# Attention and two MLPs on one core: a third exponentials buffer, selects for first tiles, one bias product a bank

## The chip, the core and the metric

One core of a Trainium2 chip runs the whole program. The metric is device time in microseconds; lower is better. Engines are named as in the profile: PE (TensorE), DVE (VectorE), ACT (ScalarE), POOL (GpSimd) and SP (SyncE, which issues every load and store here).

## What is computed

Four batches, eight heads, 576 positions, head size 64. The attention is banded (128 positions back) with a linear bias; its output, 2304 tokens by 512, goes through two MLPs with 2048 hidden units, the first with a rational activation, the second with SiLU.

```python
scores = scale * np.matmul(q, k.transpose(0, 1, 3, 2))      # scale = 1/8
bias = slopes[:, None, None] * (-np.abs(rel))[None]         # slopes 2**-(h+1)
mask = (rel >= 0) & (rel < 128)
attn = softmax(where(mask, scores + bias, -1e9))
x = (attn @ v) as 2304 x 512
h = x @ w_in;  g = P(h) / (Q(h) + 1e-6);  x = g @ w_out      # P cubic, Q quadratic in |h|
h = x @ w2_in; g = h / (1 + exp(-h));     out = g @ w2_out
```

## The kernel before, in words

The 2304 tokens are 18 tiles of 128. The first MLP works on five blocks of 4, 4, 3, 4 and 3 tiles (`BLK1`). For each block the attention runs as four groups, one for each pair of heads; group `gi` is pair `gi % 4` of block `gi // 4`, so groups 0 to 3 are all that block 0 needs, and groups 4 to 7 belong to block 1.

A group goes through these steps (`group`, below). A tile of 128 queries is cut into halves of a group (two tiles each). S: PE multiplies q and k into two PSUM banks, one for each head of the pair (line 727); a band of 128 behind a tile reaches into the tile before, so the scores lie in two 128-column parts, and DVE folds them into one by a masked copy (`copy_predicated`, line 741). In block 0, apart from the first half of group 0, PE has laid the bias and the band's mask into the bank beforehand, as a product of a scaled identity and a table (`bias_mm`, line 712); there DVE takes the row maximum (line 757) and ACT the exponential (line 762). Everywhere else DVE adds a scaled table `tabs` and takes the maximum in one custom instruction (line 750), which writes the tile `e`, and ACT takes the exponential in place (line 774). A sequence's first tile (tiles 0 and 9 lie at such a start) has no tile before it and uses a variant of the table. Then come the sums' reciprocals (lines 785, 786), the normalising product on POOL or DVE (line 793), transposes by PE (line 813), masks that split the transposed weights into the own and the previous tile (lines 844 to 862, into the tile `ph`), AV by PE (line 890), and the splitting of the result into a high and a low part, `xh` and `xl`, which the MLP reads (lines 905 to 914).

`e` has `OPT['eb']` = 2 buffers and `ph` has `OPT['ptb']` = 1; the q and k tiles have 3 each. A buffer comes free when the last reader of the group that holds it is done: for `e` its transposes, for `ph` its AV.

In `step`, one of the 16 hidden slices of a block goes through `h` (lines 948 to 950), an elementwise chain on ACT and DVE, a split into `gh` and `gl`, and the second product (lines 1017 to 1019). The weights arrive as 64-bit floats and are rebuilt by ACT and DVE (lines 573 to 580), then split into a high part (`whi`, line 470 or 478) and a low part (`wlo`, line 489 on POOL). The second MLP (`phase_a`, `phase_b`) uses a scheme with seven products in place of eight on combined quarters.

The order of the instructions on every engine is made ahead of time. Each operation is given to a planner, `Plan`, with a priority, an engine or several to choose from (`'act|pool'`), a cost and what it reads and writes. `Plan.schedule` walks through planned time and picks for each engine the ready operation with the lowest priority value; buffers and PSUM banks count as resources. `SHIFTS` then moves the priorities of runs of operations, by their index in the list. The numbers in `OPT` set the priorities of whole kinds of work (`dS`, `dT`, `dA` of S, transposes and AV; `qlead` and `vlead` of loads). The engines run the resulting order and wait for each other by semaphores. Where the plan has PE idle near the start, filler matmuls of the identity are put in (`spin`, line 517; `warm`, `fill`).

## Time and profile before

| | us |
|---|---|
| median of 3 runs (lowest to highest) | 870.12 (869.34 to 870.36) |
| profiled execution, its own time | 869.87 |
| its span, first to last instruction | 868.1 |
| PE busy | 855.8 (99%) |
| DVE busy | 674.0 (78%) |
| POOL busy | 638.1 (74%) |
| ACT busy | 579.5 (67%) |

The span is the time between the first and the last instruction of the profiled execution; the execution's own time has a little around it. Busy shares of engines overlap, and they are means over stages that differ: the first 56 us (loads, the attention of block 0, no MLP yet), the first MLP with the attention of later blocks beside it up to about 500 us, and the second MLP. The granted clock of PE is 1.00 over the span. In a timeline, consecutive instructions of the same kind are merged into one row with a count, and the brackets show how long the engine had been idle and what the profile takes for the releaser.

### The profile page before, as it was taken

The page shows a single profiled execution, that of the slowest core. Times are in us where ns is not written, and L with a number is a line of the kernel's source. Part 1 is how long each engine was busy: PE and PEld are TensorE (multiplying, and loading weights), DVE is VectorE, ACT ScalarE, POOL GpSimd, SP SyncE. Part 2 cuts the span into 40 slices and gives each one's busy share as a digit, 9 for nine tenths or more (in the row PEclk, how much of TensorE's full clock was granted, in tenths as well). Part 3 has the DMA queues.
Part 4 walks back from the last instruction along what each step waited for, and adds up shares of the span by engine and source line. Part 5 has one row for each costly group of instructions (what it writes and reads, how often), then busy time and mean ns, then how long its engine had stood idle before and what let it go on. Part 6 is the DMA issues. An engine that isn't in the chain of part 4 may idle for free.

```text
span 868.1 us, 15306 instructions
## 1 busy us (share of the span) xinstructions
PE 855.8 (99%) x5082; PEld 766.2 (88%) x5082; DVE 674.0 (78%) x1336; ACT 579.5 (67%) x1235; POOL 638.1 (74%) x615
## 2 busy tenths in 40 slices
PE   8899999999999999999999999999999999999998
PEld 6677787877788998777899999999999999999998
DVE  7899988799999898998889985567855577655662
ACT  5799997799888998988889884235422355222451
POOL 5778844676889898779899666479954599744894
PEclk9999999999999999999999999999999999999999
DMA  7566674587789877976797989898888888978884
GB/s 252 170 226 202 202 274 132 169 285 253 274 322 313 304 272 262 309 275 231 267 346 237 291 285 333 302 320 281 278 278 252 289 295 282 292 246 263 249 270 164
DMA packets 80462, 228.94 MB, mean 264 GB/s; under 512 B 8192, under 2 KB 17152, under 8 KB 80384
## 3 DMA queue, kind: packets, MB, share of 16 engines
q1 hardware_dynamic: 80384, 227.98, 78.8%
q8 instruction: 40, 0.66, 0.3%
q14 instruction: 38, 0.31, 0.1%
HBM read 178.66 MB, written 49.28 MB: 263 GB/s over the span
## 4 chain that ended last, share of the span: by engine, by line
PE 79%; DVE 9%; ACT 5%; POOL 3%; issue 2%; DMA 1%; SPq 0%; POOLq 0%; DVEq 0%; ACTq 0%
PE acc L1017 6%; PE h L948 6%; PE acc L1019 5%; PE acc L1018 5%; PE h L950 5%; PE h L949 5%; PE z_b L1360 4%; PE z_b L1358 4%; PE z_b L1359 4%; PE z_a L1294 4%; PE z_a L1292 4%; PE z_a L1293 4%; PE bank_atA L890 2%; PE bank_atA L727 2%; PE bank_atB L1358 1%
## 5 line engine op out<-in xcount | busy, mean ns | idle before, releaser
L489 POOL TENSOR_TENSOR xl_b<-g,xh_b 128x384 fp32r<-128x384 f32 x87 | 97.3, 1121 | 70.9 <-DVE xh_b L474 61.2
L1017 PE MATMUL acc<-gh,wo 128*128 128x512 f32 (+1 forms) x320 | 121.5, 380 | 0.0
L1019 PE MATMUL acc<-gl,wo 128*128 128x512 f32 (+1 forms) x320 | 118.5, 370 | 0.1
L1018 PE MATMUL acc<-gh,wo 128*128 128x512 f32 (+1 forms) x320 | 117.9, 368 | 0.0
L470 ACT CAST xh_b<-g 128x384 fp32r<-128x384 f32 x137 | 70.3, 515 | 67.9 <-PE z_b L1360 41.7
L485 DVE TENSOR_TENSOR xl_b<-g,xh_b 128x384 fp32r<-128x384 f32 x81 | 86.2, 1070 | 24.2 <-ACT xh_b L470 23.3
L389 ACT ACTIVATE g<-t_a 128x384 f32<-128x384 f32 x72 | 37.9, 527 | 93.3 <-DVE t_a L382 93.3
L489 POOL TENSOR_TENSOR gl<-t,gh 128x512 fp32r<-128x512 f32 (+1 forms) x73 | 89.8, 1230 | 13.0 <-ACT gh L470 8.7
L489 POOL TENSOR_TENSOR g<-g,g 128x384 f32<-128x384 f32 x72 | 84.5, 1183 | 2.1
L948 PE MATMUL h<-xh,ws 128*128 128x512 f32 (+1 forms) x224 | 83.9, 374 | 0.1
L950 PE MATMUL h<-xh,ws 128*128 128x512 f32 (+1 forms) x224 | 82.2, 367 | 0.0
L949 PE MATMUL h<-xl,ws 128*128 128x512 f32 (+1 forms) x224 | 82.0, 366 | 0.0
L1017 PEld LDWEIGHTS acc<-gh,wo 128*128 128x128 f32 x320 | 60.0, 188 | 13.8 <-issue 5.7
L1019 PEld LDWEIGHTS acc<-gl,wo 128*128 128x128 f32 x320 | 60.0, 188 | 9.4 <-DVE gl L485 0.7
L1018 PEld LDWEIGHTS acc<-gh,wo 128*128 128x128 f32 x320 | 60.2, 188 | 6.6
L1294 PE MATMUL z_a<-xf,w2s 128*128 128x384 f32 x192 | 64.2, 334 | 0.0
L1292 PE MATMUL z_a<-xf,w2s 128*128 128x384 f32 x192 | 64.1, 334 | 0.0
L1293 PE MATMUL z_a<-xf,w2s 128*128 128x384 f32 x192 | 64.1, 334 | 0.0
L1358 PE MATMUL z_b<-xh_b,wo2s 128*128 128x384 f32 x192 | 64.1, 334 | 0.0
L1359 PE MATMUL z_b<-xl_b,wo2s 128*128 128x384 f32 x192 | 64.1, 334 | 0.0
L1360 PE MATMUL z_b<-xh_b,wo2s 128*128 128x384 f32 x192 | 64.1, 334 | 0.0
L964 ACT ACTIVATE t<-h,ab 128x512 f32<-128x512 f32 (+1 forms) x72 | 46.7, 649 | 20.4 <-PE h L950 19.9
(227 smaller groups left out, 2732.4 us busy)
## 6 DMA issues: line engine op xcount, KB each, us to landing
w2s<-forms_w SPq DMA_DIRECT2D x84, 512.0 KB, 4.6
wo2s<-forms_wo SPq DMA_DIRECT2D x84, 512.0 KB, 4.6
ws<-sc SPq DMA_DIRECT2D x64, 512.0 KB, 4.5
raw_w<-in_w SPq DMA_DIRECT2D x32, 512.0 KB, 4.9
raw_wo<-in_wo SPq DMA_DIRECT2D x32, 512.0 KB, 5.4
forms_w<-st_w SPq DMA_DIRECT2D x24, 512.0 KB, 5.5
forms_wo<-st_wo SPq DMA_DIRECT2D x24, 512.0 KB, 4.7
sc<-w SPq DMA_DIRECT2D x16, 512.0 KB, 5.6
```

The source lines that it names most:

```text
L489: nc.gpsimd.tensor_tensor(out=o, in0=a, in1=b, op=op)
L948: nc.tensor.matmul(o, lhsT=T[W][:, 0, c], rhs=xh, start=kt == 0, stop=False)
L949: nc.tensor.matmul(o, lhsT=T[W][:, 0, c], rhs=xl, start=False, stop=False)
L950: nc.tensor.matmul(o, lhsT=T[W][:, 1, c], rhs=xh, start=False, stop=kt == KD - 1)
L1017: nc.tensor.matmul(a, lhsT=T[WO][:, 0, c], rhs=T[G1][:, :n], start=first_f, stop=False)
L1018: nc.tensor.matmul(a, lhsT=T[WO][:, 1, c], rhs=T[G1][:, :n], start=False, stop=False)
L1019: nc.tensor.matmul(a, lhsT=T[WO][:, 0, c], rhs=T[G2][:, :n], start=False, stop=last_f)
L1292: nc.tensor.matmul(o, lhsT=w(0, kt * P), rhs=x[:, 0, kt], start=st and kt == 0, stop=False, skip_group_check=True)
L1293: nc.tensor.matmul(o, lhsT=w(0, kt * P), rhs=x[:, 1, kt], start=False, stop=False, skip_group_check=True)
L1294: nc.tensor.matmul(o, lhsT=w(1, kt * P), rhs=x[:, 0, kt], start=False, stop=kt == 1, skip_group_check=True)
L1358: nc.tensor.matmul(o, lhsT=w(0, m * P), rhs=h, start=st and q == 0, stop=False, skip_group_check=True)
L1359: nc.tensor.matmul(o, lhsT=w(0, m * P), rhs=l, start=False, stop=False, skip_group_check=True)
```

## The change

`e` gets a third buffer. Its 4 KB a partition are taken from `tabs`, which held four tables a head and now holds three: the variant for first tiles goes. Where the fused add read that variant, a first tile's scores are now set to -1e30 outside the own triangle by one more masked copy (a constant column added to `lnb`), and the ordinary table is added. The order of the tables in the input changes with it, so that the product that lays bias and mask into a bank can be one matmul of 512 columns for each head instead of one of 256 for each tile. The first loads of q and k become separate operations. The choices of engines, the numbers in `OPT` and the whole list `SHIFTS` are set anew.

```diff
-    'wlo': 'pool',
+    'wlo': 'dve|pool',
...
-    'eb': 2,
+    'eb': 3,
...
-    'tabs': 'pool',
+    'tabs': 'act|pool',
...
-    'dS': -1.447,
-    'dT': 0.007,
-    'dA': 0.316,
+    'dS': -1.436,
+    'dT': 0.056,
+    'dA': 0.277,
...
-    'look': 1.601,
+    'look': 0.404,
...
-    'dg': -0.473,
+    'dg': -2.41,
...
-    'warm': 3,
+    'warm': 4,
...
-    'vlead': -0.148,
-    'qlead': 0.132,
+    'vlead': 6.85,
+    'qlead': 39.155,
...
-    'alt': 2,
+    'alt': 0,
...
-    's1': 'act|dve',
+    's1': 'act',
...
-    'th': 'act|dve',
+    'th': 'act|dve|pool',
...
-    'idn': 'dve',
+    'idn': 'pool',
...
 SHIFTS = [
-    (4, 3, -0.36), (50, 1, -0.49), (163, 60, 0.42), (297, 3, 0.9),
...
+    (31, 6, 0.69), (73, 20, -0.43), (172, 55, 0.56), (250, 20, 0.18),
...
@@ -499,8 +500,8 @@
         ident = const.tile([P, P], F32, name="ident")
         na = const.tile([P, 4], F32, name="na")
         ab = const.tile([P, 2], F32, name="ab")
-        lnb = const.tile([P, 2], F32, name="lnb")
-        tabs = tab_p.tile([P, H, 4, P], F32, name="tabs")
+        lnb = const.tile([P, 3], F32, name="lnb")
+        tabs = tab_p.tile([P, H, 3, P], F32, name="tabs")
         tabr = tab_p.tile([P, 2, 2, P], F32R, name="tabr")
         slope = tab_p.tile([P, HP, P], F32R, name="slope")
 
@@ -508,6 +509,7 @@
         make_identity(nc, ident)
         nc.vector.memset(lnb[:, 0:1], C * 2.0 ** -63)
         nc.vector.memset(lnb[:, 1:2], -LN2_63)
+        nc.vector.memset(lnb[:, 2:3], -1e30)
 
     pl.op(-99, "pool", 600, k_ident, writes=[("ident", 0), ("lnb", 0)])
 
@@ -530,8 +532,8 @@
             pl.op(-91.0 + 0.5 * part, "sp", 1150, lambda cols=cols: nc.sync.dma_start(tab_all[:, cols], table[:, cols]), writes=[("tab", part)])
         for part in range(2):
             for h in range(H):
-                pl.op(-70 + 0.1 * h + 10 * (h // 2) + 25 * part, do_copy("act" if h + part == 0 else OPT["tabs"], 2 * P,
-                      lambda h=h, part=part: (tabs[:, h, 2 * part:2 * part + 2], tab[:, 4 * part:4 * part + 2]), scale=-8.0 * 2.0 ** -(h + 1)), 0, None,
+                pl.op(-70 + 0.1 * h + 10 * (h // 2) + 25 * part, do_copy("act" if h + part == 0 else OPT["tabs"], (1 + part) * P,
+                      lambda h=h, part=part: (tabs[:, h, part:1 + 2 * part], tab[:, (1, 4)[part]:(2, 6)[part]]), scale=-8.0 * 2.0 ** -(h + 1)), 0, None,
                       reads=[("tab", part)], writes=[("tabs", h, part)])
         for hh in range(2):
             pl.op(-80.5 + 0.1 * hh, do_copy(("dve", "act")[hh], 2 * P, lambda hh=hh: (tabr[:, hh], tab[:, 0:2]), scale=0.5 ** hh), 0, None, reads=[("tab", 0)], writes=[("tabr", hh)])
@@ -623,7 +625,7 @@
 
 
     FIRST = (0, 9)
-    TABLE = {0: 1, 9: 1, 4: 2, 13: 2, 5: 3, 14: 3}
+    TABLE = {0: 0, 9: 0, 4: 2, 13: 2, 5: 3, 14: 3}
     blk_start = [sum(BLK1[:i]) for i in range(len(BLK1))]
     groups = [(bi, hp) for bi in range(len(BLK1)) for hp in range(HP)]
     xkey = {}
@@ -642,15 +644,16 @@
 
         if gi == 0:
 
-            def first(lo, hi):
+            def first(tag, d, src, lo, hi):
+                if not lo:
+                    T[(tag, gi)] = qk_p.tile([P, NB1MAX + d, P], F32, tag=tag, name=f"{tag}{gi}")
+                nc.sync.dma_start(T[(tag, gi)][:, lo + d:hi + d], src[hp, :, lo * P:hi * P].rearrange("p (t c) -> p t c", c=P))
+
+            for a, (lo, hi) in enumerate(((0, 2), (2, n))):
                 for tag, d, src in (("kd", 1, kn), ("qd", 0, qn)):
-                    if not lo:
-                        T[(tag, gi)] = qk_p.tile([P, NB1MAX + d, P], F32, tag=tag, name=f"{tag}{gi}")
-                    nc.sync.dma_start(T[(tag, gi)][:, lo + d:hi + d], src[hp, :, lo * P:hi * P].rearrange("p (t c) -> p t c", c=P))
-
-            pl.op(p, "sp", 2 * DMA_TILE * 2, lambda: first(0, 2), writes=[("kd", gi, 0), ("qd", gi, 0)])
-            pl.op(p + 1.5, "sp", 2 * DMA_TILE * (n - 2), lambda: first(2, n), writes=[("kd", gi, 1), ("qd", gi, 1)])
-            pl.ops[-1].deps -= set(pl.tile_ops[("kd", gi)])
+                    pl.op(p + 1.5 * a + 0.01 * (1 - d), "sp", DMA_TILE * (hi - lo), lambda tag=tag, d=d, src=src, lo=lo, hi=hi: first(tag, d, src, lo, hi), writes=[(tag, gi, a)])
+                    if a:
+                        pl.ops[-1].deps -= set(pl.tile_ops[("kd", gi)]) | set(pl.tile_ops[("qd", gi)])
         else:
             pl.op(p, "sp", DMA_TILE * (n + pv), load("kd", qk_p, NB1MAX + 1, ks, kn), writes=[("kd", gi)])
             pl.op(p, "sp", DMA_TILE * n, load("qd", qk_p, NB1MAX, slice(0, n), qn), writes=[("qd", gi)])
@@ -708,10 +711,9 @@
             def bias_mm(S_=S_, half=half, open_s=open_s):
                 open_s()
                 for hh in range(2):
-                    for i in half:
-                        nc.tensor.matmul(T[S_[hh]][:, i % 2], lhsT=slope[:, hp],
-                                         rhs=tabr[:, hh, TABLE.get(tiles[i], 0):TABLE.get(tiles[i], 0) + 1].broadcast_to([P, 2, P]),
-                                         start=i % 2 == 0, stop=False)
+                    t_ = tabr[:, hh] if half[0] == 0 else tabr[:, hh, 1:2].broadcast_to([P, 2, P])
+                    nc.tensor.matmul(T[S_[hh]].rearrange("p t (k c) -> p t k c", c=P), lhsT=slope[:, hp],
+                                     rhs=t_.unsqueeze(2).broadcast_to([P, 2, 2, P]), start=True, stop=False)
 
             def s_mm(S_=S_, half=half, by_pe=by_pe, open_s=open_s):
                 if not by_pe:
@@ -734,7 +736,7 @@
 
                 pl.op(pH - 0.4 * w, do_copy(OPT["qs"], len(half) * P, q_scaled, scale=0.125), 0, None, reads=[("qd", gi, a)] if gi == 0 else [("qd", gi)],
                       writes=[("qd", gi, a)])
-                pl.op(pH - 0.01 * w, "pe", 60 + 2 * len(half) * c_pe(2 * P), bias_mm, reads=[("tabr", 0), ("tabr", 1), ("slope", hp)], writes=list(S_))
+                pl.op(pH - 0.01 * w, "pe", 30 + 2 * c_pe(4 * P), bias_mm, reads=[("tabr", 0), ("tabr", 1), ("slope", hp)], writes=list(S_))
             pl.op(pH, "pe", 210 + sum(c_pe4(P if k0[i] else 192) for i in half), s_mm, reads=[("kd", gi, a), ("qd", gi, a)] if gi == 0 else [("kd", gi), ("qd", gi, a) if by_pe else ("qd", gi)], writes=list(S_))
             if two:
                 for hh in range(2):
@@ -742,12 +744,19 @@
                         T[S_[hh]][:, two, c1], tab[:, 2:3].bitcast(U32).broadcast_to([P, nt_, P]), T[S_[hh]][:, two, 0:P]),
                         reads=[("tab", 0)], writes=[S_[hh]])
 
+            for i in half:
+                if k0[i] and not by_pe:
+                    for hh in range(2):
+                        pl.op(pH + (0.021 + 0.005 * hh) * w, "dve", c_dve(P), lambda hh=hh, S_=S_, i=i: nc.vector.copy_predicated(
+                            T[S_[hh]][:, i % 2:i % 2 + 1, c1], tab[:, 2:3].bitcast(U32), lnb[:, 2:3].unsqueeze(2).broadcast_to([P, 1, P])),
+                            reads=[("tab", 0), ("lnb", 0)], writes=[S_[hh]])
+
             def mx(i, hh, S_):
                 if M_ not in T:
                     new_ml()
                 if E_ not in T:
                     new_et()
-                nc.vector.tensor_tensor_reduce(out=T[E_][:, i, hh], in0=T[S_[hh]][:, i % 2, c1], in1=tabs[:, 2 * hp + hh, TABLE.get(tiles[i], 0)],
+                nc.vector.tensor_tensor_reduce(out=T[E_][:, i, hh], in0=T[S_[hh]][:, i % 2, c1], in1=tabs[:, 2 * hp + hh, max(TABLE.get(tiles[i], 1) - 1, 0)],
                                                scale=-0.125, scalar=3.0e38, op0=ALU.add, op1=ALU.min, accum_out=T[M_][:, i, hh:hh + 1])
 
             if by_pe:
@@ -776,7 +785,7 @@
 
             parts = [(i, hh) for hh in range(2) for i in half]
             for j, (i, hh) in enumerate(parts):
-                pl.op(pH + (0.05 + 0.005 * j) * w, "dve", c_dve(P) + 8, lambda i=i, hh=hh, S_=S_: mx(i, hh, S_), reads=[S_[hh], ("tabs", 2 * hp + hh, TABLE.get(tiles[i], 0) // 2)],
+                pl.op(pH + (0.05 + 0.005 * j) * w, "dve", c_dve(P) + 8, lambda i=i, hh=hh, S_=S_: mx(i, hh, S_), reads=[S_[hh], ("tabs", 2 * hp + hh, TABLE.get(tiles[i], 1) // 2)],
                       writes=[E_ + (i, hh), M_ + (i, hh)] + ([L_ + (99,)] if i == 0 and hh == 0 else []))
             for j, (i, hh) in enumerate(parts):
                 pl.op(pH + (0.1 + 0.01 * j) * w, "act", c_act(P, False, 2), lambda i=i, hh=hh: ex(i, hh), reads=[E_ + (i, hh), M_ + (i, hh)],
@@ -1477,7 +1486,7 @@
         ok[row:, :cols] = False
         tabs.append(np.where(own, np.where(ok[:, P:], rel[:, P:], far), np.where(ok[:, :P], rel[:, :P], far)))
 
-    masks = np.ascontiguousarray(np.stack(tabs[:2] + [~own, own.T] + tabs[2:], axis=1), dtype=np.float32).reshape(P, 6 * P)
+    masks = np.ascontiguousarray(np.stack(tabs[1::-1] + [~own, own.T] + tabs[2:], axis=1), dtype=np.float32).reshape(P, 6 * P)
     coef = np.concatenate([np.asarray(inputs["moe_a"]), np.asarray(inputs["moe_b"])])
     table = np.zeros((P, 7 * P), dtype=np.float32)
     table[:, :6 * P], table[:, 6 * P:6 * P + 6] = masks, coef
```

## Rows read from the trace of the kernel before

**Rows 1.** Busy time by stretch: us and count for each engine, clock, DMA.

```profile
core 0: us, PE busy (x) PEld busy (x) DVE busy (x) ACT busy (x) POOL busy (x), PEclk, DMA share, GB/s
8.00:44.00 36.00, 31.40 (x330) 22.66 (x333) 28.88 (x94) 26.43 (x101) 25.93 (x28) 1.00 0.67 215
44.00:60.00 16.00, 14.70 (x108) 11.39 (x101) 14.07 (x32) 15.32 (x35) 12.62 (x11) 1.00 0.62 217
60.00:500.00 440.00, 439.20 (x2530) 364.22 (x2529) 399.68 (x858) 384.02 (x804) 342.91 (x346) 1.00 0.77 261
...
29.80:36.00 6.20, 5.78 (x66) 4.13 (x58) 6.20 (x28) 5.49 (x24) 3.48 (x4) 1.00 0.30 64
```

**Rows 2.** Busy time of line 517's fillers alone, 0 to 56 us.

```profile
0.00:56.00 56.00, 12.52 (x78) 10.88 (x78) 1.00 0.70 228
```

**Rows 3.** Timeline of PE: start us, us, line, tiles, count.

```profile
19.40 1.74 PE L890 MATMUL av<-ph,vh 128*64 128x256 f32 x16 [0.33 <-POOL ph L845]
...
28.48 0.72 PE L712 MATMUL bank_acc<-tabr,slope 128*128 128x256 f32 x4
...
29.04 0.60 PE L813 MATMUL bank_acc<-ident,e 128*128 128x128 f32 x4
...
29.58 0.88 PE L727 MATMUL bank_acc<-kd,qd 64*64 64x192 f32 x16
...
30.35 0.54 PE L727 MATMUL bank_atA<-kd,qd 64*64 64x192 f32 x2
...
31.57 1.73 PE L890 MATMUL av<-ph,vh 128*64 128x256 f32 x16
...
37.52 1.74 PE L890 MATMUL av<-ph,vh 128*64 128x256 f32 x16
...
41.67 1.99 PE L890 MATMUL av<-ph,vh 128*64 128x256 f32 x16
...
44.40 0.50 PE L948 MATMUL h<-xh,w 128*128 128x512 f32 x1
```

**Rows 4.** Timeline of DVE; idle time ahead and its releaser in brackets.

```profile
9.51 0.43 DVE L741 COPY_PREDICATED bank_atA<-tab,bank_atA 128x256 f32<-128x256 uint32 x1 [2.12 <-PE bank_atB L727]
...
15.66 0.69 DVE L858 TENSOR_TENSOR ph<-bank_acc,tab 128x512 f32<-128x512 f32 x1 [0.72 <-PE bank_acc L813]
...
22.12 1.52 DVE L793 TENSOR_TENSOR e<-e,l 128x512 f32<-128x512 f32 x1
...
24.73 0.68 DVE L858 TENSOR_TENSOR ph<-bank_acc,tab 128x512 f32<-128x512 f32 x1
...
29.78 0.29 DVE L750 CUSTOM_DVE_ANT_0 e<-bank_atA,tabs 128x128 f32<-128x128 f32 x1 [2.92 <-POOL ph L844]
...
33.71 0.69 DVE L858 TENSOR_TENSOR ph<-bank_acc,tab 128x512 f32<-128x512 f32 x1
...
39.66 1.29 DVE L858 TENSOR_TENSOR ph<-bank_acc,tab 128x512 f32<-128x512 f32 x2 [0.56 <-PE bank_acc L813]
```

**Rows 5.** Timeline of ACT.

```profile
25.78 0.59 ACT L470 COPY ph<-bank_acc 128x512 f32<-128x512 f32 x1
```

**Rows 6.** Timeline of POOL.

```profile
12.87 2.04 POOL L793 TENSOR_TENSOR e<-e,l 128x512 f32<-128x512 f32 x2 [2.23 <-DVE l L786]
...
23.06 1.72 POOL L910 TENSOR_TENSOR xl<-xf,xh 128x512 fp32r<-128x512 f32 x1
...
25.66 2.10 POOL L793 TENSOR_TENSOR e<-e,l 128x512 f32<-128x512 f32 x2 [0.88 <-DVE l L786]
...
27.72 1.28 POOL L844 TENSOR_TENSOR ph<-ph,tab 128x512 f32<-128x512 f32 x1
...
29.08 1.27 POOL L845 TENSOR_TENSOR ph<-ph 128x512 f32<-128x512 f32 x1
```

**Rows 7.** DVE groups by line and form, 0 to 60 us: total, mean ns.

```profile
L741 DVE COPY_PREDICATED bank_atA<-tab,bank_atA 128x128 f32<-128x128 uint32 x2 | 0.6, 297 | 0.3 <-PE bank_atB L727 0.3
```

**Rows 8.** POOL groups by line and form, 0 to 60 us.

```profile
L489 POOL TENSOR_TENSOR w<-raw_w,w 128x512 fp32r<-128x512 f32 x5 | 6.5, 1306 | 1.7 <-DVE l L786 1.4 <-ACT w L470 0.2
```

More of the change, by code (lines that the diff above doesn't have):

```diff
@@ L51 @@
     'vb': 3,
-    'tabs': 'pool',
+    'tabs': 'act|pool',
     'stb': 3,
     'strb': 3,
-    'wpro': 0.275,
-    'dS': -1.447,
-    'dT': 0.007,
-    'dA': 0.316,
-    'dm': 0.448,
-    'look': 1.601,
-    'pw': -0.699,
-    'pwo': -1.038,
-    'dg': -0.473,
-    'lead': 2.487,
+    'wpro': 0.682,
+    'dS': -1.436,
+    'dT': 0.056,
+    'dA': 0.277,
+    'dm': 0.442,
+    'look': 0.404,
+    'pw': -0.822,
+    'pwo': -1.15,
+    'dg': -2.41,
+    'lead': 2.503,
     'slk': 0,
-    'warm': 3,
+    'warm': 4,
     'fill': 0.6,
@@ L70 @@
     'ob': 3,
-    'pl': 4.452,
-    'vlead': -0.148,
-    'qlead': 0.132,
+    'pl': -1.55,
+    'vlead': 6.85,
+    'qlead': 39.155,
     'keen': 9999.0,
@@ L86 @@
     'xl03': 'd',
-    'alt': 2,
+    'alt': 0,
     'gh0': 'act|dve',
     'gl0': 'dve|pool',
-    'la': 9.598,
-    'lb': 82.219,
-    'dm2': 1.121,
+    'la': 13.632,
+    'lb': 35.361,
+    'dm2': 2.869,
     'sums': 'pool',
@@ L99 @@
     'xfl': 'dve|pool',
-    's1': 'act|dve',
+    's1': 'act',
     'tsum': 'pool',
-    'th': 'act|dve',
+    'th': 'act|dve|pool',
     'tl': 'dve|pool',
-    'tlead': -1.264,
-    'hlead': 4.083,
+    'tlead': 0.596,
+    'hlead': -0.72,
     'oq': 'sp',
-    'pw2': 35.636,
-    'rw2': 104.309,
-    'pwo2': 1023.264,
-    'rwo2': 6.486,
-    'xlead': -14.154,
-    'slead': 0.46,
+    'pw2': 31.523,
+    'rw2': 27.902,
+    'pwo2': 238.553,
+    'rwo2': 2.587,
+    'xlead': -1.162,
+    'slead': 2.482,
     'shift': 'act',
```

13 rows, old and new, of the table SHIFTS are left out of this document.

## The prediction

> **What bounds the kernel now.** I read the busy time by stretches first. From 60 to 500 us PE is busy 439.20 of 440 us, while from 8 to 44 us it idles 4.6 us and from 44 to 60 us 1.3 us [rows 1]. To the idle time at the start the filler matmuls of line 517 have to be added: 78 of them, 12.52 us busy before 56 us [rows 2]. So the bound is PE's own work from about 56 us on, and ahead of that a chain of attention groups that PE sits out. The first MLP can begin when the first four head pairs (groups 0 to 3) have their outputs xh and xl; its first matmul is at 44.40 [rows 3]. What brings that forward shortens the run about one for one, since a packed queue of PE stands behind it; what changes elsewhere is nearly always hidden.
>
> **What sets 44.40.** Next I read the timelines of that stretch. Each group passes its masks (DVE L858 and L862, or POOL L844 and L845, into the tile ph, of which there is one buffer) and then AV (PE L890, which frees ph). From the first mask to the end of AV, group 0 takes 15.66 to 21.14, 5.5 us; group 1 24.73 to 33.30, 8.6 us; group 2 33.71 to 39.26, 5.5 us; group 3 39.66 to 43.66, 4.0 us [rows 3, 4]. From group 1 on each follows the one before within 0.4 us, so this is the chain that ends at 44.40. Group 1 is 3.1 us longer than its neighbours, and the rows show on what. Its second pair of masks is POOL's. The copy that it reads ends at 26.37 [rows 5], but POOL is normalising both halves of group 2 (from 25.66, 2.10 us) and starts the mask at 27.72, 1.35 us late [rows 6]. The masks end at 30.35 [rows 6], but PE's fixed order has S of group 4 there, and AV starts at 31.57 [rows 3]: 1.2 us more.
>
> Why group 2 stands ahead of group 1's mask fits the two e buffers: groups 2 and 4 share one. DVE idles 2.92 us ahead of group 4's first write to e, at 29.78 [rows 4]. The row names POOL L844 as the releaser, but that mask was done by 29.0 [rows 6]; what ends just ahead of 29.78 is group 2's last transposes (29.04, 0.60 us) [rows 3], which release the buffer.
>
> **The change, part by part.**
>
> *Third e buffer.* In a ring of three, group 4 takes group 1's buffer, and group 1's transposes are over before its masks start. The 2.92 us hole goes. If the order stays, little comes of it: group 4's four L750 move into the hole, what is late next is S of group 3's second half (29.58, 0.88 us), then AV of group 1 (to 33.30); group 2's masks start at most 0.4 us earlier [rows 3, 4]. If the order is cut anew, with group 2 no longer urgent, POOL's mask comes 1.35 us earlier and AV need not stand behind S of group 4, 1.2 us. Ends: 0.4 and 3.1 us (group 1 as short as its neighbours). I take 1.35 + 1.2 = 2.5 us, nearer to the upper end because every priority and shift is set anew together with the buffer count, and both delays are mere places in a queue.
>
> *One bias product a bank.* 28 matmuls of 256 columns become 14 of 512. A group of four takes 0.72 us [rows 3]; the columns stay, so only the starts of 14 matmuls go. No row shows the 512-column form of this line. Bounds: nothing, and half of each of the seven groups, 7 x 0.36 = 2.5 us of PE. Since the columns stay I take 0.1 us.
>
> *Selects for first tiles.* There are ten: two for tile 0 in group 0 (its first half alone lacks the preset bias) and eight for tile 9, in the third block. The nearest rows are the selects of the same line and width, 0.29 us each [rows 7]. The two put off group 0's first exponentials by at most 0.6 us, and DVE idles 2.12 us soon after, ahead of 9.51 [rows 4]: hidden. The eight cost DVE at most 8 x 0.29 = 2.3 us in the stretch from 60 to 500, where it has 40 us idle behind a full PE [rows 1]: hidden, and 2.3 us if that cover is gone at their place.
>
> *Scaled table, slope copies, loads.* Half of POOL's work for seven heads of the first table part goes, and ACT may take more of it; POOL's next work waits 2.23 us for DVE, ahead of 12.87 [rows 6], so nothing. The slope copies move from DVE to POOL, ahead of that same idle time and of DVE's 2.12 us [rows 4]: nothing. The first q and k loads become four separate operations, and by their priorities SP issues the second k load ahead of the second table part and the second q load behind it; no load is put off against before, and what DVE waits for ahead of 9.51 is PE: nothing. The value 'alt' 2 or 0 picks the same banks, as the index a // 2 is 0 for both halves.
>
> *New order and engine choices.* The low halves of the weights may now go to DVE. On POOL one takes 1.31 us [rows 8]; on DVE the nearest rows of its width take 0.69 us (L858, one input in PSUM) and 1.52 us (L793, both inputs in SBUF) [rows 4]. Where POOL is late that wins up to 1.31 us, on a full DVE it loses up to 1.52; I take nothing. Elsewhere a new order may win what PE idles in 44 to 60, 1.3 us [rows 1], or lose as much; nothing again.
>
> POOL's subtraction L910, of the same width as the 1.28 us mask L844, takes 1.72 us while DVE's L793 is running [rows 4, 6]. The Trainium skill (Perfetto Trace Analysis, section Optimizing Scalar/DVE Operations) warns that GpSimd and DVE share a read port, so that moving work between the two might not help; the trace agrees with that, and by it the low halves on DVE become the third rival.
> The same page (section Optimization Strategy) says that a gap which repeats on the engine that should be full can mean too few buffers. In 60 to 500 PE has no such gap, 0.80 us in all [rows 1]; by that rule a third buffer gives nothing in the long middle, and the sum has nothing there.
>
> **Sum.** 2.5 + 0.1 = 2.6 us. The profiled execution took 869.87 us (span 868.1 and 1.8 us around it), 0.25 us under the median of 870.12. From the profile 867.3; as a median 867.5 us.
>
> **Rivals.**
> First, no change: the hole closes, but the order of POOL and PE around group 1 stays, and 0.4 us comes out. For it: the single ph buffer chains the groups whatever e does, and from 29.8 to 36 DVE is busy 6.20 of 6.20 us [rows 1], so work moved out of the hole only makes way for other work. Against it: the delays of group 1 are not DVE's. 869.7 us.
> Second, more: the 3.6 us between group 0's AV (21.14) and group 1's first mask (24.73) close too, since ACT and DVE may put group 1's softmax ahead of group 2's. For it: DVE normalises half of group 1 only at 22.12, 1.52 us [rows 4]. Against it: that is group 1's own work. All of it: 870.1 - 2.6 - 3.6 = 863.9 us.
> Third, slower: low halves on DVE inside the mask chain. From 29.78 on the masks are DVE's, and it is full; each such subtraction there puts off a mask by up to its 1.52 us and POOL's work beside it by 0.44 us (1.72 less 1.28). POOL does five for w before 60 us [rows 8]; three of them moved cost 3 x 1.96 = 5.9 us, 867.5 + 5.9 = 873.4 us. It decides from two on (3.9 us, more than the 2.6 gained).
>
> **How the numbers follow.** Forecast 0.47, more 0.10, no change 0.23, slower 0.20. Under 0.2% (1.7 us) cannot be told from no change, and so: faster 0.57, same 0.23, slower 0.20. The range, 863.2 to 872.6, takes in the forecast, the second rival and no change, and the start of the third. The forecast's own is 865.7 to 868.4: the 3.1 us bound with the 1.3 us of the order elsewhere, and the least gain that counts as faster.
>
> **What would show it.** Right: no DVE idle ahead of group 4's first L750; group 1 near 6 us from first mask to end of AV; the first L948 near 41.9, and all later marks 2.5 us earlier; PE in 60 to 500 as full as now. Wrong: the first L948 at 44 or later, or low-half subtractions of DVE between the masks, or new PE waits on DVE where the selects for tile 9 are.

## The result, and the profile after

| | before | after |
|---|---|---|
| median of 7 runs (lowest to highest), us | 870.76 (869.34 to 871.51) | 874.78 (872.50 to 879.26) |
| ratio after / before | | 1.0051 [1.0031, 1.0071] |
| profiled execution, us (span) | 869.87 (868.1) | 872.50 (870.7) |

The kernel got slower by 0.5%, outside the range forecast. Line numbers moved: S L727 is now L729, AV L890 is L899, the first MLP's h L948 is L957, its acc L1017 is L1026, the fused maximum L750 is L759, and L750 is now the new select. The profiled execution after is the fastest of its seven, so its trace shows 2.6 of the 4.0 us between the medians. Three of the seven (874.78, 877.02 and 879.26) have a mean granted clock of 0.998, the other four 1.00.

Busy time by stretch, after, for [rows 1]:

```profile
core 0: us, PE busy (x) PEld busy (x) DVE busy (x) ACT busy (x) POOL busy (x), PEclk, DMA share, GB/s
8.00:44.00 36.00, 31.71 (x324) 22.10 (x321) 30.27 (x98) 27.06 (x107) 25.27 (x24) 1.00 0.61 202
44.00:60.00 16.00, 14.36 (x111) 10.99 (x110) 14.43 (x40) 15.65 (x39) 10.41 (x10) 1.00 0.75 280
60.00:500.00 440.00, 436.65 (x2495) 360.26 (x2494) 401.45 (x856) 382.66 (x799) 330.62 (x335) 1.00 0.76 258
```

PE lost 2.55 us in 60 to 500, where it had been full. The fillers [rows 2] hardly changed: 80 of them, 13.05 us.

The first h came earlier, as forecast. Timeline of PE after, for [rows 3], with the first acc:

```profile
18.17 1.73 PE L899 MATMUL av<-ph,vh 128*64 128x256 f32 x16 [0.60 <-POOL ph L854]
...
28.91 1.73 PE L899 MATMUL av<-ph,vh 128*64 128x256 f32 x16
...
42.14 0.50 PE L957 MATMUL h<-xh,w 128*128 128x512 f32 x1
...
50.25 1.95 PE L899 MATMUL bank_atA<-ph,vh 128*64 128x256 f32 x20 [0.80 <-POOL ph L860]
52.13 1.38 PE L519 MATMUL bank_acc<-ident 128*128 128x128 f32 x10
54.27 0.37 PE L729 MATMUL bank_atA<-kd,qd 64*64 64x192 f32 x1 [0.76 <-DVE xl L923]
...
59.41 0.50 PE L1026 MATMUL acc<-gh,wo 128*128 128x512 f32 x1
```

The same stretch of before, from group 4's AV on:

```profile
53.90 1.95 PE L890 MATMUL bank_atA<-ph,vh 128*64 128x256 f32 x20 [1.28 <-POOL ph L851]
55.87 0.50 PE L948 MATMUL h<-xh,w 128*128 128x512 f32 x1
58.81 0.37 PE L727 MATMUL bank_atA<-kd,qd 64*64 64x192 f32 x1
59.62 0.50 PE L1017 MATMUL acc<-gh,wo 128*128 128x512 f32 x1
```

The first h comes 2.26 us earlier (42.14 against 44.40), the first acc only 0.21 us (59.41 against 59.62). Of the 2.05 us between, 0.8 us is work done sooner (half a group's S, at 54.27, now stands ahead of the third slice's h), and 1.2 us is lost.

To see where the rest went I counted each matmul with the time that its kind takes in a full queue, and compared the times at which two traces had done the same work. Negative is ahead of before (one profile each; offsets in us):

| at (us) | 44 | 57 | 200 | 240 | 500 | 860 |
|---|---|---|---|---|---|---|
| after | -2.12 | -0.94 | -0.81 | +1.38 | +3.26 | +2.80 |
| after again (e1) | -1.67 | -0.48 | -0.87 | +1.74 | +3.72 | +3.18 |

The lead of 2.1 us is halved at 44 to 57, kept to 200, then 2.2 us are lost within 40 us and 1.9 us more to 500; the second MLP from 540 on is as before. Such offsets hold to about 1 us: from 57 to 200 us e2 and e9 run the same order, and e2's trace loses nothing there, e9's 0.9 us. What PE waited for, after, from 60 to 545 us (waiting line, releaser: us, times, longest), beside before, where only 0.6 us of h L948 and 0.5 us of L1292 stand:

```profile
PE bank_atA L729 <- DVE xl L923: 1.4, 2, 1.0
PE z_a L1301 <- ACT t_a L471: 0.8, 1, 0.8
PE h L957 <- DVE t L1002: 0.6, 1, 0.6
PE acc L1028 <- POOL gl L490: 0.5, 3, 0.2
...
```

The first and third lie at 204 to 232 us and end at DVE. The selects for tile 9 are there. DVE's timeline after, the new L750 alone, and below it the POOL instructions that run beside the slow ones:

```profile
108.95 0.81 DVE L750 COPY_PREDICATED bank_atA<-tab,lnb 128x128 f32<-128x128 uint32 x1
111.07 0.28 DVE L750 COPY_PREDICATED bank_atB<-tab,lnb 128x128 f32<-128x128 uint32 x1
...
195.88 1.32 DVE L750 COPY_PREDICATED bank_atA<-tab,lnb 128x128 f32<-128x128 uint32 x1
...
214.34 1.01 DVE L750 COPY_PREDICATED bank_atA<-tab,lnb 128x128 f32<-128x128 uint32 x1
215.67 1.12 DVE L750 COPY_PREDICATED bank_atB<-tab,lnb 128x128 f32<-128x128 uint32 x1
```

```profile
108.29 1.32 POOL L490 TENSOR_TENSOR gl<-t,gh 128x512 fp32r<-128x512 f32 x1
...
195.74 1.30 POOL L490 TENSOR_TENSOR gl<-t,gh 128x512 fp32r<-128x512 f32 x1 [0.62 <-ACT gh L471]
...
213.87 1.32 POOL L490 TENSOR_TENSOR wo<-raw_wo,wo 128x512 fp32r<-128x512 f32 x1
215.34 1.29 POOL L490 TENSOR_TENSOR gl<-t,gh 128x512 fp32r<-128x512 f32 x1 [0.15 <-ACT gh L471]
```

A select takes 0.28 to 0.29 us when POOL does nothing beside it. Each slow one ends 0.15 to 0.16 us after POOL's subtraction does (109.76 after 109.61, 197.20 after 197.04, 215.35 after 215.19, 216.79 after 216.63): it stood until that instruction was over. The older masked copy (L743) of the same operation and width has its data in PSUM; after's trace has 32 of them, 15 begin while a POOL subtraction or product runs, and none takes over 0.30 us. The eight selects for tile 9 take 6.0 us (sum of the eight durations, those at 138.01 and 139.19 being 0.86 and 0.29) where 2.3 were forecast.

### The profile page after: what moved, and what is told of

The parts are those of the page before. It is cut to its first block, busy times and chain, and to the rows that moved or that the text cites. A ratio compares the mean times of both kernels' runs of the same rounds, so it can differ in the third digit from the quotient of the medians.

```text
span 870.7 us, 15298 instructions
## 1 busy us (share of the span) xinstructions
PE 855.9 (98%) x5070; PEld 764.5 (88%) x5070; DVE 654.7 (75%) x1296; ACT 590.8 (68%) x1271; POOL 633.7 (73%) x630
## 4 chain that ended last, share of the span: by engine, by line
PE 81%; DVE 7%; ACT 6%; POOL 3%; DMA 2%; issue 1%; SPq 0%; ACTq 0%; POOLq 0%; DVEq 0%
PE acc L1026 6%; PE acc L1028 6%; PE acc L1027 6%; PE h L957 5%; PE h L959 5%; PE h L958 5%; PE z_a L1301 4%; PE z_a L1303 4%; PE z_b L1369 4%; PE z_b L1368 4%; PE z_a L1302 4%; PE z_b L1367 4%; PE bank_atA L899 2%; PE bank_atA L729 2%; PE bank_atB L1369 1%; PE bank_atA L1303 1%
## 5 line engine op out<-in xcount | busy, mean ns | idle before, releaser
L1026 PE MATMUL acc<-gh,wo 128*128 128x512 f32 (+1 forms) x320 | 121.8, 381 | 0.2 <-ACT x L471 0.2
L471 ACT CAST xh_b<-g 128x384 fp32r<-128x384 f32 x133 | 68.0, 514 | 67.0 <-PE z_b L1369 43.8
L490 POOL TENSOR_TENSOR xl_b<-g,xh_b 128x384 fp32r<-128x384 f32 x83 | 91.4, 1106 | 11.2 <-ACT xh_b L471 7.3
L490 POOL TENSOR_TENSOR gl<-t,gh 128x512 fp32r<-128x512 f32 (+1 forms) x67 | 81.3, 1214 | 14.2 <-ACT gh L471 12.6
L957 PE MATMUL h<-xh,ws 128*128 128x512 f32 (+1 forms) x224 | 84.0, 375 | 0.7 <-DVE t L1002 0.6
L1026 PEld LDWEIGHTS acc<-gh,wo 128*128 128x128 f32 x320 | 60.0, 188 | 14.8 <-issue 5.6
L987 DVE SCALAR_TENSOR_TENSOR t<-t,ab,h 128x512 f32<-128x512 f32 (+1 forms) x72 | 50.3, 699 | 9.6 <-ACT t L979 7.0
```

The lines of the kernel that those rows point to most:

```text
L490: nc.gpsimd.tensor_tensor(out=o, in0=a, in1=b, op=op)
L957: nc.tensor.matmul(o, lhsT=T[W][:, 0, c], rhs=xh, start=kt == 0, stop=False)
L1026: nc.tensor.matmul(a, lhsT=T[WO][:, 0, c], rhs=T[G1][:, :n], start=first_f, stop=False)
```

## The experiments

All times are medians; e1 to e4, e5 to e8, e9 to e12 and e13 to e16 each shared one set of runs of before (870.64, 870.45, 870.41 and 870.47 us).

**e1, after unchanged.** 874.19 us, ratio 1.0040 [1.0026, 1.0054].

> The changed kernel once more, unaltered. Theory (the loss sits in places of the fixed order): the same stretches give time back at equal PE work against the kernel before, 200 to 232 us and 440 to 500 us, about +2 and +1.5 us, after a lead of about 2 us at 44 us; median 873 to 876, ratio 1.003 to 1.007. Rival (chance, some executions are merely slow): the stretches that lose differ from profile to profile, and the best run is within 1 us of the kernel before.

Its trace loses at the same places (table above), so they are the kernel's own and not one execution's. The best run, 871.60, is within 1 us of before, as the rival had it; the median is not.

**e2, an add in place of the later selects.** Order kept; the mask comes from a table filled once.

```diff
-nc.vector.copy_predicated(x, tab[:, 2:3].bitcast(U32), lnb[:, 2:3]...)
+nc.vector.tensor_tensor(out=x, in0=x, in1=T["far"], op=ALU.add)   # groups 8 to 11
+# T["far"] = tab[:, 0:1], set once to -1e30 * tab[:, 2:3]
```

> The changed kernel with its order kept; for tile 9 the select (mask and constant both read from SBUF) is an addition of a table, which reads one operand from SBUF and one from PSUM. Theory A (the select collides with POOL on the way to SBUF): the first-tile instruction falls from 0.73 to 1.23 us between starts to 0.2 to 0.3 us, the stretch 200 to 232 us loses at least 1 us less, the median is 1 to 2.5 us under that of the changed kernel run beside it. Rival B (the new order itself loses it): the instruction gets short, the stretch loses as much as before, the median stays within 0.6 us. Rival C (the read is slow in itself, whatever POOL does): the addition takes as long as the select.

872.96 us, 1.0027 [1.0018, 1.0036]: 1.23 us under e1. DVE by line in 100 to 230 us (count | busy us, mean ns):

```profile
L754 DVE TENSOR_TENSOR bank_atB<-bank_atB,tab 128x128 f32<-128x128 f32 x4 | 1.2, 294 | 0.0
L754 DVE TENSOR_TENSOR bank_atA<-bank_atA,tab 128x128 f32<-128x128 f32 x4 | 1.2, 294 | 0.0
```

The add reads one operand from PSUM and keeps to 0.29 us, also at 195.93, 213.83 and 214.43, where POOL subtracts as before. From 200 to 222 us it loses nothing where after loses 1.7. So the select's price was its two SBUF operands beside POOL. As a time that price is less sure, since the intervals of e1 and e2 overlap. But the lead goes later now (+0.07 at 240, +3.79 at 500). The waits on gl have grown to 1.9 us in 60 to 545 (5, longest 0.7); in one of them POOL stood behind a store and then took gl:

```profile
325.88 0.62 POOL L479 TENSOR_SCALAR st_w<-sums_w 128x512 fp32r<-128x512 f32 x1 [1.20 <-DMA forms_w<-st_w]
326.46 1.01 POOL L490 TENSOR_TENSOR gl<-t,gh 128x384 fp32r<-128x384 f32 x1
...
327.53 0.44 PE L1036 MATMUL acc<-gl,wo 128*128 128x384 f32 x1 [0.74 <-POOL gl L490]
```

**e3, the new structure with the numbers of before.**

```diff
 # before's OPT and SHIFTS; 'eb': 3, three tables, select, bias product and masks of after
```

> The third buffer, the smaller table, the selects and the wide bias product, planned with the priorities, shifts, engine choices and first loads of the kernel before. Theory (the numbers that were set anew lose the time from 400 us on and part of that at 200): ratio 0.998 to 1.002, nothing lost after 400 us. Rival (the new instructions lose it wherever they stand): 872 us or more. By the prediction's own step the DVE hole ahead of group 4 is gone here too, and the first L948 counterpart comes 0.4 us earlier or more.

879.09 us, 1.0094 [1.0082, 1.0106], 5 us above after. With this structure the old numbers are worse, not better. The time lies in the rival's range, but planning again reorders everything, so it is not shown that the new instructions lose it. DVE no longer idles ahead of group 4's first maximum, and yet the first h is at 44.09, only 0.31 us earlier than before: that is the prediction's first rival, with its 0.4 us.

**e4, less to rebuild.** The first six weights of w1 and wo1 are rebuilt on 32 of 512 columns, the rest of their values left out.

> The changed kernel with its order kept; rebuilding the weights of the first six hidden slices of the first MLP works on 32 of 512 columns, so ACT and DVE have some 2 to 4 us less to do between 40 and 57 us (that part of the computation is left out). Theory (the 2.2 us won by 44 us are given back by 57 us because ACT and DVE are full there and the first slice's elementwise chain takes longer): the first product of the second weights comes at least 1.5 us earlier than 59.4 us. Rival (PE's order gives them back, waiting for the attention group's xl and for its fillers): it stays within 0.5 us of 59.4.

871.51 us, 1.0010 [0.9999, 1.0021]. First acc at 57.77, 1.64 us before after's, as the theory asked; but 1.12 us of that was there at the first h (41.02), and from first h to first acc it takes 16.75 us, where after takes 17.27 and before 15.22.

**e5 to e7, the order of before from a cut on.** Three cuts in e2's plan. All that has not begun by the cut follows in before's order and on its engines.

```diff
     pl.schedule(...)
+    rest = set(THEN)               # every operation after the cut, in before's order
+    pl.seq = [o for o in pl.seq if o.idx not in rest] + [pl.ops[i] for i in THEN]
+    for i, e in zip(THEN, ON):     # ON: before's engine for each
+        pl.ops[i].eng = e; pl.ops[i].cost, pl.ops[i].fn = pl.ops[i].alts[e]
```

> The kernel of e2 (after, with the add in place of the later selects) up to what its plan puts before 44 us; from there every operation in the order and on the engine that the kernel before has, each add just ahead of the first read of its scores. So the third buffer and the new order of the beginning stand alone. Theory (the beginning is 1.7 to 2.3 us ahead at the first h, the first slice's element-wise work takes a part of that back at 50 to 57 us, and the rest of the loss is the new order of the later work): the lead at 57 us is 0.9 to 1.6 us and stays to the end, 869.0 to 869.7 against 870.6 before. Rival (a lead at the front is worth nothing, because some later resource sets the end whatever the order): 870.4 to 870.9. Second rival (the adds and the third buffer cost wherever they stand): 871.5 to 873.

> As the run before, but the order of after is kept to 60 us of the plan, past the first accumulations, and the order of before follows. Theory: the lead at 57 us is that of after, 0.5 to 0.9 us, nothing is lost later: 869.7 to 870.1. If 44 to 60 us is where the new order itself gives the lead back, this is 0.5 to 1 us above the run before; if the amount of work there does it, the two are within 0.4 us.

> The kernel of e2 with its own order to 225 us of the plan, past the last add, and the order of the kernel before from there. Theory (what e2 lost after 240 us, some 3 us at equal work, is the new order of the later work, with the second block's weights prepared on GpSimd in front of the low halves that the matmuls wait for): lead 0.4 to 0.8 us at 225 and at 500, 869.8 to 870.4. Rival (the loss after 240 us comes with the structure, whatever the order): 872 to 873.5, as e2.

All three miss every range that they were given. e5 877.28 us (1.0073 [1.0060, 1.0087]) and e7 877.92 us (1.0088 [1.0075, 1.0102]) say nothing of the orders as times: each has one stall at its seam, 5.0 us of AV for POOL's mask at 52 us, and in e7 this:

```profile
PE bank_atA L856 <- DVE xl L1058: 5.6, 1, 5.6
```

But e7 stands at +8.06 at 240 and +7.95 at 500: before's order loses nothing there. e6 took 872.75 us (1.0025 [1.0015, 1.0035]). It also loses nothing after 240 (+3.31, at 500 +3.11), but 3.0 us between 57 and 240, where the only work that before lacks is the adds. PE waits 1.8 us there for DVE ahead of h. Its busy time in 60 to 200 (before 139.44):

```profile
60.00:200.00 140.00, 138.31 (x714) 107.29 (x715) 125.14 (x248) 121.00 (x234) 93.95 (x87) 1.00 0.63 210
```

**e8, cheaper preparation of the second block.** On e2, order kept; most low halves of the second block's forms become zeros, so their values are left out.

```diff
-T[Z][:, a:b, 1] = v() - T[Z][:, a:b, 0]        # 256 columns
+... 16 columns of it, memset(0.0) for the other 240
```

> The kernel of e2, order kept, with the low halves of the second block's weight forms taken on 16 of 256 columns and a memset for the others, which leaves out most of that computation (some 0.3 to 0.6 us less on GpSimd or VectorE for each of them). Theory (this preparation standing ahead of the low halves of g on GpSimd is what TensorE waits for at 326 and 454 to 491 us): the loss between 240 and 500 us falls from 3 us to under 1.5, 871 to 871.8, and the runs lie closer together. Rival (another wait takes their place, or the loss is at the adds of the first block on VectorE): 872.5 to 873.3, as e2.

871.53 us, 1.0016 [1.0005, 1.0026]. The loss from 240 to 500 falls from 3.7 us (e2) to 0.9, as the theory has it; the runs don't lie closer together (870.26 to 874.00).

**e9, a cut without a stall, at 215 us.**

> As e7, but cut at 215 us of the plan, where no matmul is left waiting for scores that the other order makes later (e7 lost 7.2 us at that seam, at 237 us, and nothing from 240 to 500 us). Own order of e2 to 215 us, the order of the kernel before from there. Theory (what e2 loses after 240 us is the new order of the later work): the offset at equal work is the same at 240 and at 500 us within 0.5 us, and the time is 870.5 to 871.6, with e2 at 873. Rival (the loss comes with the structure): 872.5 to 873.5.

871.00 us, 1.0005 [0.9994, 1.0017]: offset +1.77 at 240, +1.59 at 500. Busy time from 240 to 500 us, of e2 and of e9:

```profile
240.00:500.00 260.00, 257.84 (x1536) 221.22 (x1535) 234.05 (x497) 226.96 (x480) 211.32 (x219) 1.00 0.81 282
```

```profile
240.00:500.00 260.00, 260.00 (x1556) 225.12 (x1555) 236.38 (x506) 225.00 (x480) 218.30 (x229) 1.00 0.82 285
```

The loss after 240 us was the order of the later work, 1.7 us as a time (2.32 over before in e2, 0.59 here).

**e10 and e11, no mask on DVE at all.** On e9 and on e6: groups 8 to 11 don't read the second variant, so its slot holds the first tiles' table for that while.

```diff
+# ScalarE, behind the last exponential of groups 7 to 10 (col 0) and 9 to 12 (col 4)
+nc.scalar.activation(out=tabs[:, h, 1:2], in_=tab[:, col:col + 1], func=AF.Copy, scale=-8.0 * 2.0 ** -(h + 1))
-in1=tabs[:, 2 * hp + hh, max(TABLE.get(tiles[i], 1) - 1, 0)]
+in1=tabs[:, 2 * hp + hh, 1 if tiles[i] == 9 else max(TABLE.get(tiles[i], 1) - 1, 0)]
```

> e9, and the later selects are gone: before groups 8 to 11, ScalarE writes the scaled table of first tiles into the slot of the second variant, which these groups don't read, and writes the variant back behind them (16 copies of 128 columns in all); nothing stands on VectorE in their place. Theory (the masking of first tiles costs on VectorE, which is full from 57 to 215 us): what e9 loses there, 0.5 to 1.5 us, is kept, 869.6 to 870.6, at or under before. Rival (ScalarE's copies cost as much as the adds, or the loss there is the order's): as e9 within 0.4 us.

> e6 (order of before from 60 us of the plan), with the slot rewritten on ScalarE in place of the adds on VectorE. From 60 us on nothing but the 16 copies on ScalarE is not in the kernel before. e6 lost 3.0 us between 60 and 240 us. Theory (those were the eight adds, 0.29 us each on a full VectorE): it loses under 0.8 us there and ends at 869.6 to 870.8, where e6 had 872.75. Rival (the third buffer, the longer queue or the seam lose it): 872 to 873.

e10: 870.49 us, 1.0008 [0.9996, 1.0019], not to be told from before, nor from e9: neither its theory nor its rival is decided, and both profiles lose 1.2 us from 57 to 240. e11: 871.09 us, 1.0013 [1.0002, 1.0024], 1.66 us under e6 (the two intervals overlap) and a little above its own range; it loses 1.2 us from 57 to 240, somewhat more than the 0.8 expected, where e6 loses 3.0. ScalarE's copies in e10 from 60 to 240 us, and e11's PE from 60 to 200 (e6: 138.31):

```profile
L922 ACT ACTIVATE tabs<-tab 128x128 f32<-128x128 f32 x14 | 3.3, 302 | 0.0
```

```profile
60.00:200.00 140.00, 139.49 (x722) 108.69 (x715) 124.22 (x253) 123.54 (x246) 95.42 (x88) 1.00 0.63 212
```

The same 128 columns cost 0.30 us on ACT, twice as often. What makes up the 1.2 us that are still lost in 57 to 240, no run shows.

**e12, two buffers.** after with `'eb': 2`, planned again.

> after with two buffers for the exponentials in place of three, planned again with the same numbers. Prediction's step (the third buffer lets the masks of group 1 go ahead of the norms of group 2 on GpSimd and VectorE go on with group 4's maxima): without it the first h is 2 to 3 us later, near 44.4, VectorE idles again for 2 to 3 us near 30 us, and the time is 1 to 3 us above after, 875.5 to 877.5. Rival (the order of the beginning does it, the buffer is not needed): first h within 0.7 us of after's 42.1, time within 1 us of after.

893.48 us, 1.0263 [1.0244, 1.0282], far outside both expectations. The first h comes at 43.84, DVE idles 3.11 us ahead of 28.98, and then PE waits through the whole first MLP for its banks, longest for DVE ahead of h (10.5 us in 15 waits).

The first h is 1.7 us later than in after, and 0.4 us later than in e9 (43.46), which runs after's order there: the direction that the step says. The rest of the 19 us can't be called the price of a buffer: these numbers were set for three, and planning again with two reorders everything.

**e13 to e16, who takes the lead back between 44 and 57 us.** All on e10. e13 and e14 leave most of four weights' conversion out on ACT alone and on DVE alone, order kept; e15 and e16 keep all work and put some thirty operations between 40 and 62 us in another order.

```diff
 # e13: w3, w4, wo1, wo2
-activation(out=top(), in_=top(), ...); activation(out=low(), in_=low(), ...)
+activation(out=top()[:, :32], ...);    activation(out=low()[:, :32], ...)
 # e14: the same weights, DVE's scalar_tensor_tensor on [:, :32]
 # e15, e16: THEN begins at 40 us, with the lists of ACT, DVE and POOL permuted
```

> e10, order kept; for the weights w3, w4, wo1 and wo2 of the first block ScalarE converts 32 of 512 columns (eight operations between 42 and 57 us, some 0.6 us each; their values are left out), VectorE's and GpSimd's work stays. Theory (between 44 and 57 us the lead is given back because the first slice's element-wise chain queues on a full ScalarE): the first accumulation comes at least 1 us earlier against the first h than in e10 (17.3 us from first h to first acc there), and the lead at 57 us is above 1 us. Rival (VectorE, or the queue of TensorE behind group 4's masks, holds it): under 0.4 us earlier.

> e10, order kept; for the same four weights VectorE joins the two words of 32 of 512 columns (four operations of some 0.65 us; values left out), ScalarE's work stays. If ScalarE holds the first slice, the first accumulation comes under 0.4 us earlier against the first h than in e10; if VectorE does, over 0.8 us earlier.

> e10 with some thirty operations of ScalarE, VectorE and GpSimd between 40 and 62 us of the plan taken in another order, no work added or left out: the first slice's first element-wise operations and the copy of group 4's transposes go ahead of group 5's last exponential and of the weights' conversions. Theory (order on a full ScalarE gives the lead back, not its amount alone): first acc 0.4 to 0.9 us earlier against first h, and 869.7 to 870.2 where e10 and before are at 870.4. Rival (amount alone): as e10 within 0.3 us.

> As e15, another order of the same stretch: group 5's exponentials stay where they are, the copy of group 4's transposes goes ahead of the second operation of the first slice, and the weights' conversions behind the slices' chain. Theory: first acc 0.5 to 1 us earlier against first h, 869.6 to 870.1. Rival: as e10 within 0.3 us.

| | before | e10 | e13 | e14 | e15 | e16 |
|---|---|---|---|---|---|---|
| time, us | 870.47 | 870.49 | 870.18 | 870.41 | 873.10 | 873.92 |
| ratio, its interval | | 0.9996 to 1.0019 | 0.9994 to 1.0011 | 0.9989 to 1.0007 | 1.0012 to 1.0034 | 1.0023 to 1.0048 |
| first h to first acc, us | 15.22 | 17.30 | 17.09 | 17.27 | 18.48 | 19.36 |

My theory fell. In e13, 3.5 us less (eight operations of 0.67 us become 0.22 us) on a ScalarE that is busy 15.66 of 16 us moves the first acc by 0.2 us against the first h; less on DVE moves it by nothing. Both reorders are worse by 1.2 and 2.1 us. So the amount of work on neither engine alone takes the lead back; the order in which the first slice's chain threads through ACT, DVE and POOL matters by microseconds, and I found none that keeps the lead. Less work on both engines at once was not run.

## Why the prediction was wrong, step by step

*Third buffer: mis-sized, and near by luck.* 2.5 us forecast, 2.26 at the first h of this profile. But 0.73 us of that stood there already at DVE's masked copy of 9.51 [rows 4], which after has at 8.78. PE's first bias products, of the same columns, had taken longer in before's trace. After, then before:

```profile
6.71 0.74 PE L715 MATMUL bank_acc<-tabr,slope 128*128 128x512 f32 x2
```

```profile
6.75 1.20 PE L712 MATMUL bank_acc<-tabr,slope 128*128 128x256 f32 x4
```

e9, with after's order there, takes 1.19 us for these two and has its first h at 43.46, so this is the execution's and not the order's. From group 0's AV to the first h it takes 23.97 us in after (18.17 to 42.14) and 25.00 in before (19.40 to 44.40): the chain won 1.0 us. With the old numbers (e3) it takes 24.98, so the buffer alone won nothing of it; it took the new order too. POOL's mask of group 1 now stands ahead of its norms, where before it stood behind them [rows 6]:

```profile
24.98 1.27 POOL L853 TENSOR_TENSOR ph<-ph,tab 128x512 f32<-128x512 f32 x1 [0.55 <-ACT ph L471]
26.33 1.28 POOL L854 TENSOR_TENSOR ph<-ph 128x512 f32<-128x512 f32 x1
29.06 2.04 POOL L802 TENSOR_TENSOR e<-e,l 128x512 f32<-128x512 f32 x2 [1.45 <-DVE l L795]
```

The way there was partly another. Group 4's first maximum comes at 25.06 (before 29.78) with no idle time ahead, as forecast; but DVE idles after it all the same:

```profile
22.99 0.67 DVE L867 TENSOR_TENSOR ph<-bank_acc,tab 128x512 f32<-128x512 f32 x1
...
25.06 0.28 DVE L759 CUSTOM_DVE_ANT_0 e<-bank_atA,tabs 128x128 f32<-128x128 f32 x1
...
28.45 0.43 DVE L743 COPY_PREDICATED bank_acc<-tab,bank_acc 128x256 f32<-128x256 uint32 x1 [2.46 <-PE bank_acc L729]
```

The hole of 2.92 us is now 2.46 us and ahead of group 3's second half. Group 1 is not near 6 us from first mask to the end of AV but 7.65 (22.99 to 30.64): 0.92 us shorter, where the term had 2.5. It also began 1.74 us earlier: group 0's AV came 1.23 us earlier, and the gap behind it, which the second rival named, is 0.51 us shorter.

*"Shortens the run about one for one": the step that failed first.* Of the 2.26 us, 1.2 were gone by the first acc, before any select for tile 9 ran. Behind 44.40 I had seen a packed queue of PE; but from 44 to 60 us PE sits out the first slice's element-wise chain, and DVE's fixed order holds that chain. DVE after, then before:

```profile
51.62 0.74 DVE L987 SCALAR_TENSOR_TENSOR t<-t,ab,h 128x512 f32<-128x512 f32 x1
52.27 0.68 DVE L998 SCALAR_TENSOR_TENSOR t<-t,h 128x512 f32<-128x512 f32 x1
52.87 0.74 DVE L992 SCALAR_TENSOR_TENSOR t<-t,na,h 128x512 f32<-128x512 f32 x1
53.53 0.69 DVE L923 TENSOR_TENSOR xl<-bank_atA,xh 128x512 fp32r<-128x512 f32 x1
54.14 0.75 DVE L1000 SCALAR_TENSOR_TENSOR h<-t,na,h 128x512 f32<-128x512 f32 x1
54.92 0.69 DVE L1002 SCALAR_TENSOR_TENSOR t<-t,h 128x512 f32<-128x512 f32 x1
```

```profile
53.28 0.68 DVE L989 SCALAR_TENSOR_TENSOR t<-t,h 128x512 f32<-128x512 f32 x1
53.88 0.75 DVE L991 SCALAR_TENSOR_TENSOR h<-t,na,h 128x512 f32<-128x512 f32 x1
54.54 0.68 DVE L982 TENSOR_TENSOR t<-t,h 128x512 f32<-128x512 f32 x1
55.13 0.68 DVE L993 SCALAR_TENSOR_TENSOR t<-t,h 128x512 f32<-128x512 f32 x1
```

L998, L1000 and L1002 (before L989, L991, L993) end the first slice's chain. Up to ACT's logarithm the chain keeps its lead (49.03 against 51.28). Then, after, the second slice's L987 stands ahead of L998, and its L992 and group 4's xl stand between L998 and L1000; before, L991 follows L989 at once. The third slice's h reuses the bank that the chain reads last, and starts as the chain ends: 55.66 against 55.87. From the first h to that end it takes 13.5 us, before 11.4. In e13 to e16 the second slice's operations or xl stand in the same places, which fits that none of them gains; no run takes just these away, so this is read from the trace and not tested. What I gave as a bound there, ±1.3 us for the order, I set to nothing. The runs agree with the upper end of the loss: e10, without the selects and the later order, ends level with before.

*Selects: the term that was mis-sized, and its cover was not there.* 8 x 0.29 us were priced by [rows 7], whose instruction reads one operand from PSUM. The new one reads two from SBUF. It cost 6.0 us in place of 2.3; e2 puts the difference at 1.23 us of the kernel's time. And the cover (DVE's 40 us of idle time in 60 to 500) is a sum over the stretch: in before's order the adds alone cost 1.66 us (e6 against e11, by intervals that overlap; 3.0 against 1.2 us in the profiles); in the new order e9 and e10 can't be told apart. "2.3 us if that cover is gone at their place" was the right bound for the add; for the select DVE's own price, 6.0 us, lay beyond it. The mark that I named for being wrong, new waits of PE on DVE where the selects for tile 9 are, is what the trace shows.

The Trainium skill states this wait, in SBUF — State Buffer, section SBUF: two separate sides: GpSimd, when it reads SBUF, and a VectorE instruction with two SBUF inputs share one pair of ports, and the one that comes second waits until the other's instruction has ended. The trace agrees, with all five slow selects ending 0.15 to 0.16 us after POOL's. I had cited the sharing for the low halves and not asked it of the selects.

*New order elsewhere: mis-sized.* Nothing was taken, with 1.3 us either way from 44 to 60 us alone. The order of the later work costs 1.7 us (e2 against e9), because the second block's preparation on POOL stands ahead of the low halves of g that PE waits for (e8: with most of that preparation left out, the loss from 240 to 500 falls from 3.7 to 0.9 us).

*Right:* the bias product (two matmuls of 512 columns take 0.71 us where four of 256 took 0.72; the 2.5 us end of the bound is out). The loads and the scaled table show no cost in 0 to 44 us. The third rival, low halves on DVE, did not happen: DVE takes three low halves of the first MLP's weights, at 73, 94 and 110 us, all behind the mask chain. Its time, 873.4 us, was near by luck, for another reason.

Added up on the profiles: -2.12 at 44, +1.18 to 57, +0.13 to 200, +2.19 to 240, +1.88 to 500, -0.46 behind. As medians: 3.55 us over before (e1), of it 1.23 the select's two SBUF operands (e2, by intervals that overlap), 1.73 the later order (e9); the 0.59 us left in e9, and the 0.08 in e10, are within the noise.

*Open:* which order would free the first slice, since neither less work on ACT or DVE nor two other orders did; what is lost from 57 to 240 us without any mask on DVE; how much of the first h's lead is the kernel's, with one trace of before; and why after's runs spread over 7 us where before's spread over 2.

## What to carry to other kernels

Price an added instruction by a row with the same kinds of operands, PSUM or SBUF, not only the same width; and look who runs beside it. Idle time of an engine summed over 440 us covers nothing by itself: look at the stretch where the new work stands. A start that comes earlier is worth only what the next chain can take; follow it to the first instruction that waits for something else, in the order that each engine really runs. And measure a step of a microsecond between two marks of one chain, not from the span's start: a start that differs from execution to execution moves every later mark.

## What the runs showed of the hardware

A select of 128 columns with mask and constant in SBUF took 0.28 to 0.29 us alone and up to 1.32 us beside a POOL tensor_tensor, to whose end it was held; an add of the same width with one operand in PSUM took 0.29 us beside the same instructions, and a masked copy of that width with its data in PSUM at most 0.30 us.

One long wait of PE cost its clock too. Stretches of e7 behind its seam (PEclk is the column after POOL's):

```profile
237.00:243.00 6.00, 0.43 (x2) 0.01 (x1) 1.20 (x3) 2.46 (x5) 1.93 (x2) 0.72 0.97 356
243.00:250.00 7.00, 6.93 (x39) 5.30 (x40) 6.22 (x21) 4.26 (x13) 3.16 (x4) 0.75 0.71 220
250.00:260.00 10.00, 10.00 (x67) 7.53 (x66) 8.66 (x18) 8.25 (x16) 10.00 (x11) 1.00 0.42 143
```

PE had waited 5.6 us; the mean grant of 0.72 and 0.75 is a mix of the two levels, 1.2 and 2.4 GHz, and it was back at the full one by 250 us. The seam cost about 7 us of offset in all.

A wait of 2.1 us was followed by a fall in some executions only. Between 23 and 27 us PE waits that long for ACT's exponentials, with the same work before and behind it; PEclk from 27 to 30 us was then 0.50 in e5, e8 and e16 (the level of 1.2 GHz), and 1.00 in after and e10. Those three take 25.0 to 25.4 us from group 0's AV to the first h, where after takes 23.97.
